# Gates of four row tiles by GpSimd and ScalarE instead of TensorE, and one VectorE step ahead of another

## The chip, the cores and the metric

One core of one Trainium2 chip runs the whole program. The metric is the device time of one execution in microseconds (us). Beside the timed runs there is one profiled execution with a trace. Engines are called PE or TensorE (matmuls), DVE or VectorE, ACT or ScalarE, POOL or GpSimd, and SP, which only issues DMAs.

## The reference

Two sequence layers read the same input `x` (2048 rows of 1024 channels) and are mixed by a gate for each row:

```python
g = sigmoid((x * gate_w).sum(-1, keepdims=True))
a = A(x)      # state space layer: h = Lam_bar * h + B_bar x, y = 2 Re(C h) + x * Dskip
b = B(x, k, v)  # k shifted and weighted by 4 taps, times v, long convolution with ssm_k
                # along the rows (plus ssm_D), times x
return g * a + (1 - g) * b
```

The case is about the first line: for each of the 2048 rows, a sum of 1024 products and two sigmoids, of the sum and of its negative.

## The kernel before

The rows are cut into four blocks `tb` of 512, each of four row tiles `t_` of 128 (0 to 15). The kernel has two halves that overlap.

The first half makes layer B by transforms along the rows, a loop over `c` of eight groups of 128 channels. For each group VectorE multiplies two spectra in a generator, `products(c)`, whose steps are taken one by one with `step` and `steps`: the first step is `first(0)` into `acc`, the second `second(0)` into `wkh` with a gather `acc<-wkh`, the third `first(1)`, the fourth `second(1)`. A "gather" here is a DMA issued by GpSimd that adds its source onto its destination. Between these steps the loop runs the next group's `times_v`: its last step takes `ev = ks - lo` on VectorE and then gathers `ks<-lo`, and the transform `fwd_V` on TensorE reads `ev` and `ks`. At the end of a group `inverse` writes the result to the scratch `cv_scr`.

The second half is the state space layer. `Bu` makes TensorE's input products, `turn_U` rotates them: four ScalarE passes into `Q`, gathered in two gathers into the same tile of `U` (for one group `V`). `scan(tb, g)` runs 16 times (`j = 0..15`) on VectorE. For `j = 8` to `12` the string `plan[j]` gives the output products on TensorE: `Cy_group(tb, g)` adds group `g` into four PSUM tiles, one for each row tile, and after group 3 `scale_a` evicts each tile on ScalarE times the gate (`m<-psy` for block 1, `BT<-psy` for block 2), and `combine` gathers layer B's part onto it. There are four PSUM tiles in all, handed out in turn. The last block's output products follow the loop.

`loads(t_)` loads a row tile's part of layer B (`pbb`) and of `x` (`xr`) on SP's queue; for tiles 12 to 15 `xr` lies in `xlast`. `scale_b(t_)` is two ScalarE passes, `pbb` times `omg` and the `Dskip` row times `gcols`, and a gather. `gcols[:, t_]` holds the gate of a row tile and `omg[:, t_]` one minus it. `gate(tb)` makes them for four row tiles: 32 matmuls of one column with `xT` as weights, then two sigmoids over four columns (`gates_of`). For the last block, `gate(3)` runs at the end of `j = 7`.

What sets the order: `put` chains each instruction of an engine behind the one issued before it, so every engine (GpSimd and SP too) works in the order of the code, and the waits between engines follow from the tiles. Since nearly all instructions go through `put`, they bear its line, L95, in the profile, and are told apart by tile names.

Of the kernel before, what the change touches and what calls it, by code (L numbers as in the profile page):

```python
# [9 lines left out]
ALU = mybir.AluOpType  # L10
ACT = mybir.ActivationFunctionType
BF16 = mybir.dt.bfloat16
F32 = mybir.dt.float32
# [7 lines left out]
def kernel(  # L21
# [26 lines left out]
    nc = tc.nc  # L48
# [4 lines left out]
    S, D = xf.shape  # L53
# [14 lines left out]
    def pool(name, bufs, **kw):  # L68
        return ctx.enter_context(tc.tile_pool(name=name, bufs=bufs, **kw))

    consts = pool("consts", 1)
# [21 lines left out]
    def put(eng, f, *a, **kw):  # L93
        with tc.issue_after(prev[eng]) if eng in prev else nullcontext():
            i = f(*a, **kw)  # L95
        prev[eng] = getattr(i, "ins", i)
# [4 lines left out]
    def bc(ap, shape):  # L101
        return ap.to_broadcast(shape)
# [15 lines left out]
    def act(o, i, **kw):  # L118
        put("act", nc.scalar.activation, out=o, in_=i, **kw)
# [4 lines left out]
    def move(o, i):  # L124
        put("sp", nc.sync.dma_start, out=o, in_=i)
# [670 lines left out]
    def gates_of(c4, sums):  # L796
        act(gcols[:, c4], sums, func=ACT.Sigmoid)
        act(omg[:, c4], sums, func=ACT.Sigmoid, scale=-1.0)

    def gate(tb):  # L800
        psg = ps2([128, 2, 512], "p")[:, 0, 0:4]
        for tl in range(4):
            for dt_ in range(ND):
                mm(psg[:, tl:tl + 1], xTs[tb][:, dt_, tl * 128:(tl + 1) * 128], gwb[:, dt_:dt_ + 1],
                   dt_ == 0, dt_ == ND - 1)
        gates_of(slice(tb * 4, tb * 4 + 4), psg)
# [242 lines left out]
    ios, gas = {}, {}  # L1049
# [5 lines left out]
    def bt_row(g, i):  # L1055

        return BT[g].rearrange("p c d q -> p (c d q)")[:, i * D:(i + 1) * D]
# [60 lines left out]
    def store(t_):  # L1118
        move(rows_of(of, t_), gas.pop(t_))

    def step(gen):
        next(gen, None)

    def run(gen):
        for _ in gen:
            pass

    def steps(gen, n):
        for _ in range(n):
            step(gen)  # L1130
# [41 lines left out]
    tv = times_v(1)  # L1172
# [17 lines left out]
    for c in range(NC - 1):  # L1190
        n, nn = c + 1, c + 2
        if c == 0:
            load("kn", 2)
            load("kT", 2)
            load("v", 2)
            load_BT(0, 0)
            load_xT(0, (1,))
            p1 = products(0, 1)
            fwd_K(n, (0, 1))
            steps(p0, 2)  # L1200
            run(tv)
            dg = dgs(nn, True)
            steps(p1, 2)
            step(p0)
            step(p1)
            run(p0)
            taps(nn, dg)
            step(sp)
            fk = fold_columns(nn)
            step(fk)  # L1210
            fwd_K(n, (2, 3))
            step(p1)
            step(sp)
            fwd_V(n)
            run(p1)
            run(fk)
            tv = times_v(nn)
            step(tv)
            load("kn", 3)
            load("kT", 3)  # L1220
            load_BT(0, 1)
            apart = spread(3)
            step(apart)
            load_xT(0, (0,))
            run(apart)
            continue
        if c == 6:
            put("pool", nc.gpsimd.tensor_copy, stamp, xTs[2][:, 0, 0:HB + 1:HB])
        if c == 6:
            CT[1] = ct_pool.tile([128, 2, D], BF16, name="CT1")  # L1230
            load_CT(1)
            move(rows_, bc(A_Dskip.rearrange("(o d) -> o d", o=1), [128, D]))
        tabs, back, prod = turn_table(c - 1) if c <= NG else none, inverse(c - 1), products(c)
        step(old)
        step(tabs)
        if c == 6:
            step(parts)
        run(back)
        step(tv)
        steps(prod, 4)  # L1240
        run(tv)
        step(old)
        step(tabs)
        run(old)
        fk = none
        if nn < NC:
            dg = dgs(nn)
            if by_channel(nn):
                fk = fold_columns(nn)
                step(fk)  # L1250
        if c == 2:
            step(parts)
        fwd_K(n, (0, 1))
        if c in (2, 6):
            step(parts)
        fwd_K(n, (2, 3))
        if c == 1:
            lam_diag(0, lam_pool, True)
        if c == 4:
            step(parts)  # L1260
        if c == 6:
            run(sp)
            s5p["Q"] = s5p["wu"]
            run(turns_U[2])
            gate(0)
        step(prod)
        if nn < NC:
            if not by_channel(nn):
                fk = mirror_K(nn)
            step(fk)  # L1270
            if c < 5:
                step(fk)
            if c == 4:
                step(parts)
            if c == 1:
                load_BT(1, 0, True)
            elif c in (2, 4):
                load("v", nn, True)
            step(parts)
            taps(nn, dg)  # L1280
            if c == 5:
                load("v", nn)
                load_xT(2, held=True)
            if nn + 1 < NC:
                load("kT", nn + 1, True)
                load("kn", nn + 1)
                apart = spread(nn + 1)
                step(apart)
                if c == 1:
                    load_BT(1, 1)  # L1290
                elif c in (2, 3):
                    load_xT(1, (3 - c,))
                run(apart)
        step(prod)
        run(fk)
        run(prod)
        if n == NC - 1:
            overlap_K(n)
        if nn < NC:
            tv = times_v(nn)  # L1300
            step(tv)
            step(parts)
        else:
            run(next(tiles))
            CT[0] = ld.tile([128, 2, D], BF16, name="CTa", tag="ld")
            hold(CT[0][:, 0, 0:1])
            load_CT(0)
            load_BT(2, 0)
            load_BT(2, 1)
            run(next(tiles))  # L1310
            run(next(tiles))
        fwd_V(n, (0, 1))
        if c < 6 and c != 4:
            step(parts)
            if c in (1, 3):
                step(parts)
        fwd_V(n, (2, 3))
        if c in (4, 5):
            step(parts)
        if c == 1:  # L1320
            lam_diag(1, lam_pool)
        old = tabs

    h3r.close()
    c = NC - 1
# [81 lines left out]
    wk = pool("wk", 2)  # L1407
    s5p["io"] = pool("io", 2)
    s5p["v13"] = pool("v13", 1)

    load_CT(6)
    load_CT(7)
# [44 lines left out]
    def between(j):  # L1457
        for k in multiplied.get(j, ()):
            product(k)
        yield  # L1460
        if j == 3:
            run(turning[6])

    scans = [scan(j // NG, j % NG, between(j)) for j in range(NS)]

    def advance(j):
# [29 lines left out]
    for j in range(NS):  # L1496
        for k in loaded.get(j, ()):
            loads(k)
        if j == 7:
            store(3)  # L1500
        for k in stored.get(j, ()):
            store(k)
        advance(j)
        if j in behind:
            product(behind[j])
        for t in turning[2 * j:2 * j + 2]:
            run(t)
        if j > 0:
            on_act += [lambda t=t: step(t) for t in turning[2 * j + 2:2 * j + 4] for _ in range(4 if j == 1 else 2)]
        turn = turns_U[turned[j]] if j in turned else none  # L1510
        if j != 10 and plan[j][0:1] != "G":
            step(turn)
        by_group = plan[j][0:1] == "G" and j != 10
        if j == 7:
            scale_b(6)
        if by_group:
            for n, k in enumerate(scaled_b.get(j, ())):
                if n == 1:
                    step(turn)
                scale_b(k)  # L1520
            run(turn)
        if j == 4:
            put_off.pop()()
            scale_b(3)
        for unit in plan[j].split():
            if unit == "C0":
                scale_b(2)
            if unit[0] == "G":
                Cy_group(int(unit[1]), int(unit[2]))
            else:  # L1530
                (Bu_next if unit[0] == "B" else Cy_row)(int(unit[1:]))
        if put_off:
            put_off.pop()()
        if j == 10:
            step(turn)
            for k in scaled_b[j]:
                scale_b(k)
            run(turn)
        elif not by_group:
            run(turn)  # L1540
            if j == 5:
                run(turns_U[5])
            for k in scaled_b.get(j, ()):
                scale_b(k)
        if j == 7:
            gate(3)

    for k in at_end:
        product(k)
# [64 lines left out]
```

## Time and profile before

| | |
|---|---|
| median of 3 runs | 379.53 us (379.37 to 379.69) |
| the profiled execution | 379.12 us, of which the span is 377.3 us |
| PE busy | 370.3 us (98%) |
| DVE busy | 367.8 us (97%) |
| ACT busy | 303.9 us (81%) |
| POOL busy | 76.3 us (20%) |
| DMA packets | 70.99 MB, mean 188 GB/s |

Times in the trace are in us from the span's start. A row of a timeline gives the start, the time that it took, the engine, the line, the operation with output and inputs, shapes and count, and in brackets how long the engine stood idle before it and what ended that. A busy time of PE is modelled for pipelined matmuls, so rows overlap a little. A wait for several semaphores is put down to the one that came last by the profile; where the engine named had long been done, it was another, often a DMA. Rows of DMA issues close with the median time from issue to landing; SPq and POOLq are the queues of SP and GpSimd.

### The profile page before, as it was taken

How to read it: one execution, taken by the hardware profiler on the slowest of the kernel's cores; microseconds unless marked ns; L12 is line 12 of the kernel's file. 1: busy time of each engine (PE TensorE's matmuls, PEld its weight loads, DVE VectorE, ACT ScalarE, POOL GpSimd, SP SyncE). 2: the span in 40 equal slices, each digit the busy share in tenths (PEclk: the TensorE clock that was granted, in tenths of full speed). 3: DMA queues.
4: the chain of work that ended last, by engine and by line, in shares of the span. 5: the costliest groups of instructions: out<-in, count | busy, mean ns of one | idle time of the engine just before them, and what ended most of it. 6: DMA issues, size and time to landing. Idle time of an engine off the chain costs nothing.

```text
span 377.3 us, 6661 instructions
## 1 busy us (share of the span) xinstructions
PE 370.3 (98%) x2442; PEld 201.8 (53%) x2477; DVE 367.8 (97%) x596; ACT 303.9 (81%) x465; POOL 76.3 (20%) x106
## 2 busy tenths in 40 slices
PE   8999999999999999999999999999999999999996
PEld 5657567575674847644454444444444444444444
DVE  8999999999999999999999999999999999999975
ACT  5979998988979999687999699978879967946301
POOL 4011030120301203022012013122425323532000
PEclk9999999999999999999999999999999999999999
DMA  7889999999989879998999999746999998996223
GB/s 169 169 141 244 222 219 202 234 217 223 222 188 214 166 167 197 195 202 145 222 210 236 225 197 241 165 75 117 193 240 159 270 247 180 193 248 119 57 83 112
DMA packets 121827, 70.99 MB, mean 188 GB/s; under 512 B 98425, under 2 KB 103425, under 8 KB 121794
## 3 DMA queue, kind: packets, MB, share of 16 engines
q1 hardware_dynamic: 108416, 45.90, 54.6%
q0 software_dynamic: 12256, 24.38, 37.4%
q10 hardware_dynamic: 1122, 0.28, 0.4%
q8 instruction: 19, 0.31, 0.3%
q14 instruction: 14, 0.11, 0.1%
HBM read 16.01 MB, written 8.39 MB: 65 GB/s over the span
## 4 chain that ended last, share of the span: by engine, by line
PE 90%; issue 5%; DMA 3%; SPq 0%; POOL 0%; ACT 0%; DVE 0%; POOLq 0%; ACTq 0%
PE psy L95 29%; PE both L95 22%; PE psk L95 11%; PE psz L95 6%; PE psv L95 6%; PE taps L95 4%; PE foldk L95 4%; PE even L95 3%; PE odd L95 3%; DMA ks<-lo 2%; DMA kT<-in_B_k_dram 1%; PE p L95 1%; PE mirror L95 1%; SPq L95 0%; POOL acc L95 0%
## 5 line engine op out<-in xcount | busy, mean ns | idle before, releaser
L95 PE MATMUL psy<-CT,U 128*128 128x512 bf16 (+1 forms) x418 | 92.7, 374 | 0.4
L95 PEld LDWEIGHTS <-U 128*128 128x128 bf16 x492 | 48.1, 98 | 55.6 <-issue 0.3
L95 PEld LDWEIGHTS <-BT 128*128 128x128 bf16 x544 | 50.5, 98 | 33.5 <-issue 0.2
L95 DVE TENSOR_TENSOR wkh<-BT,Vh 128x2048 bf16<-128x2048 bf16 (+3 forms) x31 | 44.6, 1458 | 0.0
L95 POOL DMA_DIRECT2D U<-Q x26 | 26.6, 1035 | 80.6 <-ACT Q L95 33.0
L95 DVE TENSOR_TENSOR acc<-BT,Vh 128x4096 bf16<-128x4096 bf16 (+3 forms) x19 | 36.9, 1948 | 0.3 <-ACT Vh L95 0.2
L95 ACT ACTIVATE Q<-U,lam 128x512 bf16<-128x512 bf16 (+1 forms) x60 | 35.0, 626 | 1.4 <-issue 1.3
L95 PE MATMUL both<-xT,BT 128*128 128x512 bf16 x157 | 35.2, 379 | 0.2
L95 ACT ACTIVATE Vh<-psv 128x1024 bf16<-128x1024 f32 x32 | 30.6, 1033 | 5.6 <-PE psv L95 5.5
L95 DVE TENSOR_TENSOR_SCAN A<-rv,init,A 128x256 bf16<-128x256 f32 x48 | 34.4, 736 | 0.0
L95 DVE TENSOR_TENSOR acc<-acc,wkh 128x1024 bf16<-128x1024 bf16 (+4 forms) x30 | 32.7, 1128 | 0.1
L95 ACT ACTIVATE BT<-psk 128x1024 bf16<-128x1024 f32 x31 | 30.1, 1046 | 2.3 <-PE psk L95 2.2
L95 ACT ACTIVATE U<-both 128x512 bf16<-128x512 f32 x44 | 24.3, 594 | 8.1 <-PE both L95 7.8
L95 POOL DMA_DIRECT2D acc<-wkh x8 | 9.7, 1218 | 100.7 <-DVE wkh L95 100.7
L95 PEld LDWEIGHTS <-SF 128*128 128x128 bf16 x184 | 18.0, 98 | 19.6 <-issue 0.9
L95 PE MATMUL psk<-eok,SF 128*128 128x384 bf16 (+1 forms) x118 | 28.0, 354 | 0.2
L95 ACT ACTIVATE BT<-psy,gcols 128x1024 bf16<-128x1024 f32 (+1 forms) x6 | 6.3, 1043 | 25.6 <-issue 14.6
L95 PE MATMUL psz<-Vh,CI 128*128 128x512 bf16 x64 | 24.3, 379 | 0.0
L95 PE MATMUL psz<-Vh,SI 128*128 128x512 bf16 x64 | 24.3, 379 | 0.0
L95 PEld LDWEIGHTS <-kT 128*128 128x128 bf16 x352 | 21.5, 101 | 1.6 <-DMA kT<-in_B_k_dram 1.1
L95 PE MATMUL taps<-dg,kT 128*128 128x128 bf16 (+1 forms) x352 | 22.1, 212 | 0.1
L95 DVE TENSOR_TENSOR U<-U,trn 128x512 bf16<-128x512 bf16 (+1 forms) x60 | 22.0, 390 | 0.1
(225 smaller groups left out, 780.1 us busy)
## 6 DMA issues: line engine op xcount, KB each, us to landing
U<-Q POOLq DMA_DIRECT2D x26, 256.0 KB, 4.7
acc<-wkh POOLq DMA_DIRECT2D x6, 768.0 KB, 8.1
cv_scr<-cv SPq DMA_DIRECT2D x16, 256.0 KB, 3.6
kn<-in_B_ssm_k_dram SPq DMA_DIRECT2D x6, 512.0 KB, 3.9
v<-in_B_v_dram SPq DMA_DIRECT2D x2, 1024.0 KB, 6.9
out_dram<-m SPq DMA_DIRECT2D x8, 256.0 KB, 4.2
BT<-cv_scr SPq DMA_DIRECT2D x7, 256.0 KB, 6.0
out_dram<-BT SPq DMA_DIRECT2D x7, 256.0 KB, 2.0
```

Of the source, the lines that this page charges most:

```text
L95: i = f(*a, **kw)
```

## The change

Two edits.

The first is in the loop over `c`: for `c == 5`, the rest of `times_v` (that is, `ev` and the gather `ks<-lo`) runs ahead of the fourth step of `products` and not behind it.

The second takes away `gate(3)`. The row `gate_w` is loaded at the end of `j = 8`, broadcast to 128 partitions, into a room in `BT[0]` that row tile 4 used (`gw_row`). At the end of `j = 9, 10, 11, 12`, GpSimd multiplies the `x` rows of tile 12, 13, 14, 15 with it into `gx`, one f32 tile of 128x1024 that all four share. At the start of the following `j`, ScalarE copies `gx` onto itself with a sum over each row into a column of `gsum`, and `gates_of` makes that tile's two gate columns.

```diff
@@ -1237,7 +1237,10 @@
         run(back)
         step(tv)
-        steps(prod, 4)
+        steps(prod, 3)
+        if c == 5:
+            run(tv)
+        step(prod)
         run(tv)
         step(old)
@@ -1407,6 +1410,9 @@
     s5p["v13"] = pool("v13", 1)
+    gx = pool("gx", 1).tile([128, D], F32, name="gx")
+    gsum = consts.tile([128, 4], F32, name="gsum")
+    gw_row = bt_row(0, 2)
...
+    weighed = {9: 12, 10: 13, 11: 14, 12: 15}
+
     scans = [scan(j // NG, j % NG, between(j)) for j in range(NS)]
@@ -1498,6 +1506,11 @@
         if j == 7:
             store(3)
+        if j - 1 in weighed:
+            t_ = weighed[j - 1]
+            col = gsum[:, t_ - 12:t_ - 11]
+            act(gx, gx, func=ACT.Copy, accum_out=col)
+            gates_of(slice(t_, t_ + 1), col)
         for k in stored.get(j, ()):
             store(k)
         advance(j)
@@ -1542,8 +1555,10 @@
-        if j == 7:
-            gate(3)
+        if j == 8:
+            move(gw_row, bc(gate_w.rearrange("(o d) -> o d", o=1), [128, D]))
+        if j in weighed:
+            put("pool", nc.gpsimd.tensor_tensor, out=gx, in0=ios[weighed[j]][1], in1=gw_row, op=ALU.mult)
```

## The prediction

> **What bounds the kernel now.** I read the page first (busy shares, then the chain that ended last), then the timelines of the engines about the two places that are edited, then the landings of the DMAs there.
>
> ```profile
> span 377.3 us, 6661 instructions
> ...
> PE 370.3 (98%) x2442; PEld 201.8 (53%) x2477; DVE 367.8 (97%) x596; ACT 303.9 (81%) x465; POOL 76.3 (20%) x106
> ...
> PE 90%; issue 5%; DMA 3%; SPq 0%; POOL 0%; ACT 0%; DVE 0%; POOLq 0%; ACTq 0%
> ```
>
> TensorE carries the chain: whatever makes it stand, or takes work off it, moves the end one for one until another engine is late. VectorE is nearly as full. ScalarE and GpSimd have room by their sums, so it is their order, not their load, that has to be read. TensorE's timeline at three places of this case:
>
> ```profile
> 290.28 0.94 PE L95 MATMUL p<-gwb,BT 128*128 128x1 bf16 x32
> ...
> 318.86 1.03 PE L95 MATMUL psy<-CTa,U 128*128 128x512 bf16 x4
> ...
> 346.49 1.03 PE L95 MATMUL psy<-CTa,U 128*128 128x512 bf16 x4
> ```
>
> The first are the gate products that go. The second row starts output block 2 (G20), the third the last block. Each block takes all four PSUM tiles, so its first matmul needs ScalarE to have emptied the tile of row tile 4 (after G13) or 8 (after G23). Neither waits now. On VectorE, the first step that adds row tile 12 to its output:
>
> ```profile
> 366.54 1.28 DVE L95 SCALAR_TENSOR_TENSOR BT<-psy,gcols,xlast 128x1024 bf16<-128x1024 f32 x1 [1.83 <-PE psy L95]
> ```
>
> VectorE waits for TensorE at the end, with at least 1.83 us in hand.
>
> **Part 1, ev ahead of the fourth product step (c = 5).** Nothing is added; ev and then the gather ks<-lo come one product earlier, the product 0.6 us later.
>
> ```profile
> 153.07 0.59 PE L95 MATMUL psv<-ks,SF 128*128 128x512 bf16 x2 [0.84 <-DMA ks<-lo]
> ```
>
> That is the one stall of TensorE in the body, on the landing of the gather.
>
> ```profile
> 143.55 1.75 DVE L95 TENSOR_TENSOR wkh<-BT,Vh 128x3072 bf16<-128x3072 bf16 x1
> 145.22 0.68 DVE L95 TENSOR_TENSOR ev<-ks,lo 128x1024 bf16<-128x1024 bf16 x1
> ```
>
> ```profile
> 141.73 1.20 POOL L95 DMA_DIRECT2D acc<-wkh  x1 [14.97 <-DVE wkh L95]
> 146.21 0.90 POOL L95 DMA_DIRECT2D ks<-lo  x1 [3.27 <-PE psk L95]
> ```
>
> ```profile
> acc<-wkh POOLq DMA_DIRECT2D x1, 768.0 KB, 8.8
> ks<-lo POOLq DMA_DIRECT2D x1, 256.0 KB, 6.8
> ```
>
> The gather would be issued at 146.21 - 1.67 = 144.54. The transfer in front of it in GpSimd's queue lands at 141.73 + 8.8 = 150.5, and the gather at 146.21 + 6.8 = 153.0, 2.5 us after: it stands behind 768 KB either way. The gain lies between 0 and the 0.84 us of the stall; I take 0.1. It counts only if nothing later stops TensorE for longer.
>
> **Part 2a, what goes.** The 32 one-column products of gate(3): 0.94 us of TensorE at 290.28, on the chain, and two small sigmoids. Their PSUM tile also leaves the rotation, which lengthens the distance of the following tiles from their last user: nothing lost. By itself this is -0.94 us.
>
> **Part 2b, what comes, and where it stands.** Four GpSimd products of 128x1024 into one f32 tile gx, four ScalarE sums over it, eight one-column sigmoids, one 256 KB load of gate_w. In the changed order, the product of tile 12 stands on GpSimd behind the second V<-Q gather at j = 9, and its sum on ScalarE stands **ahead of the four m<-psy evictions of block 1**. The products of 13 and 14 stand behind the second U<-Q at j = 10 and 11; the sum of 14 and then scale_b(14) stand ahead of the four evictions of block 2. ScalarE is in order, so those evictions, and TensorE behind them, wait for gathers.
>
> ```profile
> 313.88 1.11 ACT L95 ACTIVATE m<-psy,gcols 128x1024 bf16<-128x1024 f32 x1 [0.41 <-PE psy L95]
> ```
>
> ```profile
> 310.51 1.50 POOL L95 DMA_DIRECT2D V<-Q  x1
> ...
> 319.45 0.86 POOL L95 DMA_DIRECT2D V<-Q  x1 [6.43 <-ACT m L95]
> ```
>
> ```profile
> DMA to landing us min/median/max: 3.3/5.9/8.4
> ```
>
> (The last line is of the two V gathers.) ScalarE is through with the turn at 313.88 - 0.41 = 313.47 and then evicts. But the second V<-Q is not issued before 319.45. The wait named there, ScalarE's m, cannot be it: 310.51 + 8.4 = 318.91, the landing of the first V gather into the same tile, is 0.54 us before it.
>
> The price of a product: no such instruction is in the trace. The nearest GpSimd rows:
>
> ```profile
> 0.98 0.55 POOL L271 IOTA fr__i<- 128x512 int32 x1
> ...
> 2.19 0.46 POOL masks.py:199 TENSOR_SCALAR_AFFINE_SELECT ident<-ident 128x128 bf16<-128x128 bf16 x1
> ```
>
> The DMA share (last but one column) ahead of the first V gather, and one of the sigmoids:
>
> ```profile
> 305.00:310.00 5.00, 4.95 (x23) 2.25 (x23) 5.00 (x13) 2.58 (x4) 0.61 (x2) 1.00 1.13 237
> ```
>
> ```profile
> 295.35 0.19 ACT L95 ACTIVATE gcols<-p 128x4 f32<-128x4 f32 x1
> ```
>
> Twice the iota (written only) is 1.1 us; eight times the select (read and written) is 3.7. I take 2.2, a little over the geometric middle (2.0): two operands are read, but the fixed part of the select is counted eight times. A sum costs one pass of 1.1 us, and two sigmoids with the wait between about 0.35: 1.45 together. The load of gate_w meets full DMA engines (share 1.13, 237 GB/s): 256 KB are 1.1 us, between 0 and that for the first V gather; I take 1.1.
>
> First stall: V gather issued 319.45 + 1.1 + 0.86 = 321.4; product to 323.6; sum and gates to 325.05; eviction 1.11, to 326.15. TensorE wants this tile at 318.86: **+7.3 us**.
>
> Second stall. The U gathers of the next two scans, their landings (300 to 360 us), and ScalarE's passes of such a scan:
>
> ```profile
> 332.60 0.86 POOL L95 DMA_DIRECT2D U<-Q  x1 [6.99 <-ACT Q L95]
> ...
> 333.68 1.62 POOL L95 DMA_DIRECT2D U<-Q  x1
> ...
> 342.17 0.86 POOL L95 DMA_DIRECT2D U<-Q  x1 [5.98 <-issue]
> ```
>
> ```profile
> DMA to landing us min/median/max: 3.4/7.2/9.9
> ```
>
> ```profile
> 320.07 1.32 ACT L95 ACTIVATE Q<-U,lam 128x512 bf16<-128x512 bf16 x2
> 321.30 1.14 ACT L95 ACTIVATE row<-row,omg 128x1024 bf16<-128x1024 bf16 x1
> 322.34 1.13 ACT L95 ACTIVATE gd<-rows,gcols 128x1024 bf16<-128x1024 bf16 x1
> ```
>
> Before, 332.60 - 319.45 = 13.15 us pass for six gathers, V, four m, U, 2.2 each. Now the four m and U follow from 326.15 on: U's landing lets the second U<-Q go at 337.15 and be issued at 338.0. Product 13 to 340.2, sum and gates 341.7, scale_b(12) with two passes of 1.04 to 343.8, the first turn of U15 1.23 to 345.0. The next second gather came 342.17 - 333.68 = 8.5 us after the first as third of four; now it is second of two, 3.4 at least: I take 5.2, so it is issued at 350.25 + 0.86 = 351.1. Product 14 to 353.3, sum and gates 354.75, scale_b(14) 356.85, eviction 357.95. TensorE wants that tile at 346.49, and with the first stall it comes at 353.8: the two stalls make **+11.5 us**. The 0.94 and the 0.1 only make it arrive earlier at the first stall and are lost there.
>
> The products on GpSimd may also hold VectorE: 4 x 2.2 = 8.8 us at most, none at least. TensorE's lateness of 11.5 covers it, with 1.83 on top. VectorE's other tie:
>
> ```profile
> 352.96 0.66 DVE L95 TENSOR_TENSOR U<-U,Q 128x1024 bf16<-128x1024 bf16 x1
> ```
>
> Its Q comes from ScalarE and now follows three more evictions, sum 15 and scale_b(15): 357.95 + 3.3 + 1.45 + 2.1 + 1.2 = 366.0, or +13.0, less the 1.83 in hand +11.2: just under TensorE.
>
> The profiled execution took 379.12 us (377.3 of span, 1.8 around it), 0.41 below the median of 379.53. 379.53 + 11.5 = **391.0 us**.
>
> Bounds: with 1.1 a product, no delay from gate_w and the quickest landings, the second stall falls to +3.7, and the first, +5.1, decides: 384.6. With 3.7 a product (+4.5 over three) and 8.5 for the last gather (+3.3): 398.8.
>
> The Trainium skill, "SBUF — State Buffer", section "Who interferes with whom", says that a VectorE instruction with two SBUF inputs and a GpSimd instruction that reads SBUF exclude each other for a whole instruction. No run shown here has such a pair; by that rule VectorE would lose the whole 8.8 us, and each product would first wait out a VectorE instruction.
>
> **Rivals.** (a) Only the first stall counts: landings are quick once the queue is less full, products cheap, and TensorE meets its second tile free: +5 to +9, at 386.5. For it: the shortest landings, 3.3 and 3.4; against: the medians 5.9 and 7.2.
>
> (b) Longer: each product has to get in between VectorE's back-to-back instructions, such as the 0.66 us U<-U,Q, and the stalled TensorE restarts slowly. Three products wait 0.7 each, 2.1.
>
> ```profile
> 1.19 1.46 PE L95 MATMUL raised<-wkh 128*128 128x512 bf16 x3 [1.19 <-DVE magic L95]
> ```
>
> Three 512-column matmuls at the start, after idleness, take 1.46 us, four in the body 1.03; if about 3 us run so, 1.6 us are lost after the last stall. Together +15.2: 394.7; with dearer products to 400. The page "TensorE: Matmul & The Clock Gate" of the Trainium skill, Part 1, has the same: half rate after an idle window, for one busy window of about 3.4 us.
>
> (c) Faster: ScalarE finds the sum's input ready, nothing stalls, 0.94 to 1.78 us are saved: 378.2 in the middle. That needs product 12 done by 313.47, so the second V gather issued by 310.4, before the first (310.51). It speaks against itself unless the first gather lands in quite another way.
>
> (d) ScalarE unhurt as in (c), but VectorE held for 8.8 us: it has 1.83 in hand before the last block, and TensorE would come 0.94 sooner: 8.8 - 1.83 = 7.0, so 386.5 at most, from 1.83 us of holding on.
>
> (e) The gates end up hidden, stall against saving: no change.
>
> **How the numbers follow.** Forecast (388 to 393) 0.45; (a) 0.21; (b) 0.24; (c) 0.05; (d) 0.03; (e) 0.02. About 0.2% (0.8 us) is what a measurement of this kernel can tell from no change. Faster 0.05, same 0.02, slower 0.93. The range 384 to 398.5 takes in the forecast, (a), (d) and most of (b), and leaves out (c), (e) and the dear end of (b).
>
> **What would show it.** In the profile after: TensorE's first psy matmuls of blocks 2 and 3 with idle time before them, ended by ScalarE's m and BT; ScalarE idle for some 9 us after the turn of Q<-O, released by a GpSimd product of gx; that product starting right after the second V<-Q at about 321; ks<-lo still landing near 153. The forecast is wrong if the product of tile 12 is done before 314, or if TensorE doesn't stand before block 2; its size is wrong if a product takes far from 2.2 us, or if the second block finds its tile free.

## The result and the profile after

| | before | after |
|---|---|---|
| median of the runs beside each other | 379.55 us (6 runs) | 393.24 us (6 runs) |
| the profiled execution | 379.12 us, span 377.3 | 393.92 us, span 392.1 |

The ratio is 1.0336, 95% interval 1.0308 to 1.0364. Here and below, ratios leave disturbed (slow) executions out, so they need not be the quotient of two medians, and the traces of part 1 alone (both) and of the kernel with `gate(0)` moved are of such executions.

Lines of the page of after, and TensorE's waits of the whole run (in total, times, longest):

```profile
span 392.1 us, 6656 instructions
...
PE 373.9 (95%) x2445; PEld 201.3 (51%) x2445; DVE 376.8 (96%) x596; ACT 308.7 (79%) x479; POOL 85.5 (22%) x110
...
DVE 49%; issue 14%; PE 11%; DMA 10%; SPq 7%; ACT 5%; POOL 3%; POOLq 0%; DVEq 0%; ACTq 0%
```

```profile
PE psy L95 <- ACT m L95: 8.0, 1, 8.0
PE psy L95 <- ACT U L95: 2.2, 1, 2.2
PE psy L95 <- ACT BT L95: 1.6, 1, 1.6
PE psv L95 <- DMA ks<-lo: 1.5, 1, 1.5
```

Before, `psy` waited for no one; now it waits 11.8 us. VectorE's busy time is 9.0 us longer with the same 596 instructions. The chain of waits, 90% TensorE before, now is a mixture. TensorE's timeline at the starts of blocks 1, 2 and 3 (before: 291.08, 318.86, 346.49):

```profile
293.49 1.03 PE L95 MATMUL psy<-CTa,U 128*128 128x512 bf16 x4
...
329.30 1.87 PE L95 MATMUL psy<-CTa,U 128*128 128x512 bf16 x4 [8.03 <-ACT m L95]
330.96 1.91 PE L95 MATMUL psy<-CT,U 128*128 128x512 bf16 x4
332.67 1.51 PE L95 MATMUL psy<-CTa,U 128*128 128x512 bf16 x4
334.02 1.03 PE L95 MATMUL psy<-CT,U 128*128 128x512 bf16 x4
...
360.84 1.02 PE L95 MATMUL psy<-CTa,U 128*128 128x512 bf16 x4 [1.62 <-ACT BT L95]
```

The last block starts 14.35 us later than before, and the last output matmuls too. So the loss is made by 360.84. What it was made of is read along GpSimd and ScalarE:

```profile
315.19 1.31 POOL L95 DMA_DIRECT2D V<-Q  x1
...
323.73 0.86 POOL L95 DMA_DIRECT2D V<-Q  x1 [5.60 <-issue]
324.29 2.45 POOL L95 TENSOR_TENSOR gx<-xlast,BT 128x1024 f32<-128x1024 bf16 x1
...
353.62 2.44 POOL L95 TENSOR_TENSOR gx<-xlast,BT 128x1024 f32<-128x1024 bf16 x1
```

```profile
326.77 1.06 ACT L95 ACTIVATE gx<-gx 128x1024 f32<-128x1024 f32 x1 [8.20 <-POOL gx L95]
...
328.16 4.11 ACT L95 ACTIVATE m<-psy,gcols 128x1024 bf16<-128x1024 f32 x4
...
356.09 1.06 ACT L95 ACTIVATE gx<-gx 128x1024 f32<-128x1024 f32 x1 [3.79 <-POOL gx L95]
...
359.69 4.11 ACT L95 ACTIVATE BT<-psy,gcols 128x1024 bf16<-128x1024 f32 x4
```

ScalarE stands 8.20 us for the product of tile 12, with four evictions that need nothing of it queued behind. The same order stands in front of block 3, where ScalarE waits 3.79 us for the product of tile 14 and then does `scale_b(14)` ahead of the evictions.

### The profile page after: what moved, and what is told of

Its sections match the earlier page's. It is cut to its first block, busy times and chain, and to the rows that moved or that the text cites. A ratio compares the mean times of both kernels' runs of the same rounds, so it can differ in the third digit from the quotient of the medians.

```text
span 392.1 us, 6656 instructions
## 1 busy us (share of the span) xinstructions
PE 373.9 (95%) x2445; PEld 201.3 (51%) x2445; DVE 376.8 (96%) x596; ACT 308.7 (79%) x479; POOL 85.5 (22%) x110
## 4 chain that ended last, share of the span: by engine, by line
DVE 49%; issue 14%; PE 11%; DMA 10%; SPq 7%; ACT 5%; POOL 3%; POOLq 0%; DVEq 0%; ACTq 0%
DVE acc L95 18%; DVE wkh L95 12%; SPq L95 7%; PE psy L95 7%; DVE Vh L95 4%; DVE A L95 3%; DVE t L95 3%; DMA xlast<-in_A_x_dram 3%; DVE ks L95 2%; DVE U L95 2%; ACT BT L95 2%; DMA BT<-cv_scr 2%; DMA m<-xr 1%; PE taps L95 1%; DMA pbb<-cv_scr 1%
## 5 line engine op out<-in xcount | busy, mean ns | idle before, releaser
L95 PE MATMUL psy<-CT,U 128*128 128x512 bf16 (+1 forms) x426 | 94.1, 376 | 0.0
L95 PEld LDWEIGHTS <-BT 128*128 128x128 bf16 x512 | 49.6, 98 | 33.2 <-issue 0.2
L95 POOL DMA_DIRECT2D U<-Q x26 | 24.0, 935 | 80.2 <-ACT Q L95 38.7
L95 DVE TENSOR_TENSOR_SCAN A<-rv,init,A 128x256 bf16<-128x256 f32 x48 | 38.6, 824 | 0.0
L95 PE MATMUL psy<-CTa,U 128*128 128x512 bf16 (+1 forms) x66 | 18.1, 396 | 11.9 <-ACT m L95 8.0
```

## The experiments

### Part 2 alone, part 1 alone

Part 2 alone is the changed kernel without the edit at `c == 5`.

> Only part 2: the gates of tiles 12 to 15 by GpSimd and ScalarE, products(5) in the order of before. If ScalarE's sums ahead of the evictions make the loss, TensorE stands 6 to 8.5 us before block 2 with ScalarE's m as releaser, restarts block 3 at 358 to 361 us, and the time is 389 to 392 us. Rival, part 1 makes a good part of the loss by its later landing: 386 to 388 us here.

Measured: 391.33 us, ratio 1.0308 (1.0274 to 1.0342). TensorE's waits for ScalarE are 8.5 us on `m` and 2.1 on `BT`, and block 3 starts at 359.54. Part 2 makes nearly all of the loss.

Part 1 alone is the kernel before with this, run in two comparisons:

```diff
-        steps(prod, 4)
+        steps(prod, 3)
+        if c == 5:
+            run(tv)
+        step(prod)
```

> Only part 1: ev and the gather ks<-lo one product earlier at c = 5; gate(3) stays on TensorE. If the gather stands in GpSimd's DMA queue behind the 768 KB of acc<-wkh, issuing it 1.67 us earlier doesn't land it earlier: it lands at 153 to 154 us, TensorE's stall stays at 0.8 to 1.5 us, and the time is 379.5 to 380.5 us. Rival, the issue time counts: the gather lands at 151.4, the stall of 0.84 us is gone, 378.7 us. Second rival, the 0.8 us later landing seen after the change is multiplied by what follows (DMA transposes, ScalarE waiting for CT<-m, 2.2 us of TensorE before the first psy): 382 us or more.

> Part 1 alone once more (ev and the gather ks<-lo one product earlier at c = 5), beside the kernel with the gather ahead of acc<-wkh. Theory: the gather lands within 1 us of 153, behind the 768 KB, and the ratio is 1.000 to 1.004. Rival (part 1 delays the rest by 2 us, as TensorE's 2.4 us of lateness before block 1 in the changed kernel would have it): ratio 1.005 or more.

Measured: ratios 1.0022 (0.9985 to 1.0059) and 1.0005 (0.9983 to 1.0027). The gather was issued some 1.5 us earlier in both, at 144.79 and 144.62; it landed at 144.79 + 9.3 = 154.1 and at 144.62 + 7.6 = 152.2, against 153.0 before. So the landing scatters about the old one though the issue is earlier each time, and no change of the time can be told. In the changed kernel the landing fell on the late side, at 144.54 + 9.3 = 153.8:

```profile
144.54 0.90 POOL L95 DMA_DIRECT2D ks<-lo  x1 [1.60 <-DVE ev L95]
```

```profile
ks<-lo POOLq DMA_DIRECT2D x1, 256.0 KB, 9.3
```

```profile
153.91 0.59 PE L95 MATMUL psv<-ks,SF 128*128 128x512 bf16 x2 [1.46 <-DMA ks<-lo]
```

### The gather ahead of the 768 KB

The kernel before, with `ev` and the gather `ks<-lo` two products earlier at `c == 5`, and issued before `acc<-wkh`:

```diff
@@ products(c)
             second(0)
+            if c == 5:
+                yield
             gather(A[:, 0, :, 1:], n1[:, 0])
@@ the loop over c
-        steps(prod, 4)
+        if c == 5:
+            steps(prod, 2)
+            run(tv)
+            step(prod)
+        else:
+            steps(prod, 2)
+        steps(prod, 2)
```

> The kernel before with one edit at c = 5: ev and the gather ks<-lo are issued two products earlier and before the 768 KB gather acc<-wkh, so that in GpSimd's queue the order of the two is turned round. Theory (GpSimd's gathers land in the order in which they stand in its queue, so part 1 could gain nothing behind the 768 KB): ks<-lo lands by 147 to 149 us instead of 153 to 154, the 0.84 us stall at 153 goes, acc<-wkh lands some 3 us later; TensorE comes up to 0.84 earlier, though the end may keep only part of it: ratio 0.998 to 1.000. Rival 1 (the gather lands late for its own sake, small rows and full DMA engines): it still lands after 152 and the stall stays. Rival 2 (acc<-wkh, now later, is waited for): a new wait on acc, 1 to 3 us, and slower by 0.3 to 0.8%.

```profile
142.50 0.86 POOL L95 DMA_DIRECT2D ks<-lo  x1 [15.88 <-DVE ev L95]
143.04 1.55 POOL L95 DMA_DIRECT2D acc<-wkh  x1
```

```profile
acc<-wkh POOLq DMA_DIRECT2D x1, 768.0 KB, 10.6
...
ks<-lo POOLq DMA_DIRECT2D x1, 256.0 KB, 5.6
```

It lands at 148.1, 5 us earlier for an issue 3.7 us earlier, and TensorE's stall at 153 is gone. That bears out the prediction's reason, the place in the queue behind 768 KB: from issue to landing the gather took 7.6 to 9.3 us behind the 768 KB with part 1, and 5.6 ahead of them. The time is still the same: 1.0009 (0.9976 to 1.0042). The interval is too wide to exclude the 0.5 us that the profile's span (376.8) shows.

### Other work in that hole

The kernel before, with `gate(0)` moved from `c == 6` into the stall:

```diff
@@ c == 6
             run(turns_U[2])
-            gate(0)
@@ ahead of fwd_V
+        if c == 5:
+            gate(0)
         fwd_V(n, (0, 1))
```

> The kernel before with one edit: the 32 one-column gate products of the first 512 rows, gate(0), and their sigmoids are issued at c = 5 in front of the backward products, where TensorE stood 0.84 us for the gather ks<-lo, instead of at c = 6. Neither gx nor the gather's place changes. Theory (the gather lands with GpSimd's queue, whatever TensorE does; what is done in the wait is free): the stall at 153 goes or shrinks to 0.1, and the time falls by 0.7 to 0.9 us, ratio 0.998. Rival 1 (TensorE's lead at c = 5 is lost at the next tie, the wait for ScalarE or VectorE by 250 us, or at the end): no change, 1.000 within 0.001. Rival 2 (the gates' PSUM tile or their sigmoids, now earlier, push a ScalarE step of that turn): slower by 0.3 to 1 us, with a ScalarE wait in the rows behind 153.

The stall is gone there too (the 32 one-column products run in it, 0.94 us), and the ratio is 0.9998 (0.9975 to 1.0021). A gain of 0.8 us would just lie within that interval; what is shown is only that it isn't larger.

### What the removal saves

The kernel before without `gate(3)`; the gates of the last four row tiles are not computed, they get those of the four tiles before.

> gate(3) is left out and nothing is put in its place: tiles 12 to 15 get the gate columns of block 2 (so the gates of the last 512 rows are not computed). Prices the removed matmuls by themselves. If they are on the chain one for one: 0.94 us less, 378.6 us. Rival, VectorE or a DMA takes the end over: 379.3 to 379.5 us.

Measured: ratio 0.9974 (0.9944 to 1.0005), so 1.0 us, uncertain by 1.2: the -0.94 of the prediction fits, though the interval just takes in no gain at all. So much, about 1 us, is to be had by taking these products off TensorE with nothing put in their place.

### The products alone

The kernel before with the load of `gate_w` and the four GpSimd products, without the sums, and with `gate(3)` kept. ScalarE's order is then as before.

> gate(3) stays and makes the gates; the load of gate_w and the four GpSimd products of part 2 are added at their places, their result is not used, and there are no sums on ScalarE. If the order on ScalarE makes the loss, TensorE doesn't stand before block 2 or 3. What is left is VectorE, held about 2 us by each product (2.0 to 2.4 us in the trace after): 8 us late at the end, of which its idle time at the end covers some 4: 381 to 384 us. Rival, the hold of VectorE is the loss: 388 us or more.

Measured: 386.81 us, ratio 1.0188 (1.0154 to 1.0222), beyond the 381 to 384 that I had expected and short of the rival's 388. In the last 90 us TensorE no longer waits for ScalarE but for VectorE, and VectorE has no wait left at the end:

```profile
PE psy L95 <- DVE U L95: 2.9, 2, 2.5
```

GpSimd's third product, and VectorE's timeline through it and the fourth:

```profile
345.06 4.60 POOL L95 TENSOR_TENSOR gx<-xlast,BT 128x1024 f32<-128x1024 bf16 x1
```

```profile
346.94 0.75 DVE L95 TENSOR_TENSOR A<-A,trn 128x512 bf16<-128x512 bf16 x2
347.61 2.47 DVE L95 TENSOR_SCALAR A<-V,lam 128x512 bf16<-128x512 bf16 x2
350.00 3.93 DVE L95 TENSOR_SCALAR trn<-V,lam 128x512 bf16<-128x512 bf16 x2
```

Each pair of `TENSOR_SCALAR` took 0.61 us before. The product issued at 345.06 waits through VectorE's back-to-back two-input instructions until 347.61, then VectorE stands until it is over. A product of 2.44 us so becomes 4.60, and VectorE loses 1.9 us (2.47 instead of 0.61). The page "SBUF — State Buffer" of the Trainium skill, section "Who interferes with whom", has this as a lock held for a whole instruction; the runs agree on VectorE's side, and show on GpSimd's that the wait can be several VectorE instructions, not one.

### One stall taken out

Part 2 alone, with the sum of tile 12 behind the evictions of block 1:

```diff
-        if j - 1 in weighed:
+        if j - 1 in weighed and j != 10:
             gate_of(weighed[j - 1])
@@ behind the last put-off eviction
+        if j == 10:
+            gate_of(12)
```

(`gate_of` is the sum and the two sigmoids.)

> Part 2 alone, with one edit: the ScalarE sum of tile 12 and its two sigmoids are queued behind the four evictions m<-psy of block 1 instead of ahead of them; the sum of tile 14 and scale_b(14) stay ahead of the evictions of block 2. Theory (one chain: GpSimd's products and gathers set when the second stall ends, and TensorE's lateness there is the larger of the two): the stall of 8 to 8.5 us before block 2 goes, but the gathers behind product 12 stay late, the stall before block 3 grows from about 2 to 5 us or more, and the time is 386 to 390 us, 2 to 5 below part 2 alone. Rival 1 (the two stalls add, each its own): the stall before block 3 stays at about 2 us and the time falls by about 8, to 383. Rival 2 (VectorE takes over): TensorE hardly waits for ScalarE any more, VectorE, held some 8 to 10 us by the products as with the products alone, is busy to the end and the time is 386 to 387 whatever the stalls do. Theory and rival 2 are told apart by what ends TensorE's waits in the last 40 us: ScalarE's BT, or VectorE's U.

Measured: 391.46 us, ratio 1.031 (1.0279 to 1.0342), just as with both stalls:

```profile
356.67 1.87 PE L95 MATMUL psy<-CTa,U 128*128 128x512 bf16 x4 [9.28 <-ACT BT L95]
...
360.03 1.05 PE L95 MATMUL psy<-CTa,U 128*128 128x512 bf16 x4
```

The stall before block 2 is gone and the one before block 3 grew from 2.1 to 9.28 us, ended by `BT` and not by VectorE. So the stalls don't add: the chain over GpSimd's gathers and products decides when block 3 may start. Block 3 starts 2.9 us earlier than with part 2 alone (359.54), but now TensorE comes out of the long idleness and takes 6.84 us for the first 24 matmuls instead of 5.17: of the 2.9 us, 1.7 are given back there, and the span falls by 1.2. My theory had the mechanism and not this; its 2 to 5 us did not come.

### The products earlier

Part 2 alone, with each product in front of the second gather of its turn:

```diff
             for k in scaled_b.get(j, ()):
                 scale_b(k)
+            if j in (9, 11):
+                weigh(weighed[j])
             run(turn)
```

(and likewise for `j = 10`; the last one stays at the end of `j = 12`).

> Part 2 alone, with the GpSimd products moved in front of the second gather of their turn (they stood behind it); the sums stay where they are on ScalarE, in front of the evictions. GpSimd stood idle for 6 to 8 us between the two gathers of a turn. Theory: product 12 ends near 321 rather than 326.7, its sum near 322.5, so the stall before block 2 falls from 8.5 to about 4 us (the gather behind it comes up to 2.4 us later only if the product isn't over by the time that it could go), the stall before block 3 stays under 2 us, and the time is 385 to 388 us, VectorE's hold of 8 to 10 us setting the floor. Rival (the wait is for VectorE, not for the queue of gathers): a product issued earlier only waits longer for an instruction of VectorE that lets it in, it ends at the same time as before and the time stays at 390 to 392 us.

Measured: 385.19 us, ratio 1.0135 (1.0097 to 1.0172).

```profile
313.34 4.22 POOL L95 TENSOR_TENSOR gx<-xlast,BT 128x1024 f32<-128x1024 bf16 x1
```

```profile
315.50 2.47 DVE L95 TENSOR_SCALAR A<-U,lam 128x512 bf16<-128x512 bf16 x2
```

```profile
PE psy L95 <- DVE U L95: 2.1, 2, 1.7
PE psy L95 <- ACT m L95: 1.8, 1, 1.8
```

Product 12 is done at 317.6 rather than 325.3, the wait on `m` falls from 8.5 to 1.8 us, that on `BT` goes, and about 6 us come back. The rival (a product only waits for VectorE longer) falls.

The next step puts the sums of 12 and 14 and `scale_b(14)` behind the evictions as well:

> As the kernel before it in this list (part 2 alone, products ahead of the second gather), and the sums of tiles 12 and 14 with their sigmoids, and scale_b(14), are queued behind the four evictions of the block instead of ahead. No eviction waits for a product any more. Theory: TensorE has no stall on ScalarE's m or BT over 1 us; what is left is VectorE, whose instructions the products hold for 8 to 10 us in sum, less the 1.83 us that it had in hand and less the 0.94 us of gate products: 379.5 + 6 = 385 to 387 us, as with the products alone (386.8) less up to 0.9. Rival (the hold of VectorE hides as long as ScalarE's order is good): 379 to 381 us, no slower than before by more than 0.5%.

Measured: 386.2 us, ratio 1.0153 (1.0108 to 1.0198). TensorE has no wait for ScalarE's `m` or `BT` left, and the time gains nothing more: VectorE bounds the end, as with the products alone.

### How much of VectorE's time a product costs

The same placement as in the kernel with 385.19 us, with products and sums over 512 columns:

```diff
-                weigh(weighed[j])
+                weigh(weighed[j], 512)
```

> Part 2 with the products in front of the second gather (385.2 us), and each product and sum over 512 of the 1024 columns; half of each of the four gates' sums is left out. Theory (what is left of the loss is VectorE standing while a product runs: 1.9 to 2.5 us for each full one, held from the moment it is let in): the products take about 1.2 us, hold VectorE 0.7 to 1.3 each, 3 to 5 us in sum instead of about 9, and the time falls by 3.5 to 5 us, to 380 to 382. Rival (each product costs VectorE a fixed price, and ScalarE its sums and sigmoids, whatever their width): less than 1.5 us better, 383.7 or more.

Measured: 381.56 us, ratio 1.0067 (1.0035 to 1.0098). `TENSOR_SCALAR` is held for less:

```profile
315.79 1.51 DVE L95 TENSOR_SCALAR A<-U,lam 128x512 bf16<-128x512 bf16 x2
```

That is 0.9 us of hold instead of 1.9, in three of the four products; the remaining one, that of tile 13, held 1.8 instead of 2.5. The hold goes with the product's length. The last control gives GpSimd the same time without reading an operand, in the products-only kernel:

```diff
-        put("pool", nc.gpsimd.tensor_tensor, out=gx, in0=ios[t_][1], in1=gw_row, op=ALU.mult)
+        for h in (0, 512, 0, 512):
+            put("pool", nc.gpsimd.iota, gx[:, h:h + 512], pattern=[[4, 512]], base=1, channel_multiplier=0)
```

> The products-only kernel (386.8 us; no sums, gate(3) kept) with each GpSimd product replaced by four iotas of 128x512 int32 into the same place, 4 x 0.55 = 2.2 us of GpSimd without any operand read; nothing uses them. Theory (a product with two operands in SBUF excludes VectorE's two-input instructions, an iota doesn't): VectorE's instructions keep their lengths, and the time is 379.5 to 381, as before but for the load of gate_w and later gathers. Rival 1 (GpSimd's time in front of the gathers is what costs): 385 to 387 as with the products. Rival 2 (any GpSimd instruction that writes SBUF holds VectorE): its instructions show holds of 0.5 us or more at the iotas, and the time is 383 or more.

Measured: 381.77 us, ratio 1.0067 (1.0041 to 1.0094), between theory and rivals.

```profile
336.50 2.21 POOL L95 IOTA gx<- 128x512 int32 x4
...
345.30 2.40 POOL L95 IOTA gx<- 128x512 int32 x4
```

```profile
336.30 1.38 DVE L95 TENSOR_TENSOR_SCAN A<-rv,init,A 128x256 bf16<-128x256 f32 x2
337.60 0.66 DVE L95 TENSOR_TENSOR U<-U,A 128x1024 bf16<-128x1024 bf16 x1
...
345.35 3.22 DVE L95 TENSOR_SCALAR A<-V,lam 128x512 bf16<-128x512 bf16 x2
```

Scans and two-input instructions beside iotas keep their lengths (1.38 and 0.66 as before); `TENSOR_SCALAR` is held for 2.6 us, and a `CAST` took 0.88 us instead of 0.16. So rival 1 (GpSimd's time as such, 385 to 387) falls as the whole price, and reading the operands is what makes most of the products' price; my theory that iotas leave VectorE alone was wrong for one kind of instruction. The section of the Trainium skill named above has both cases: two-input instructions meet only GpSimd's reads, `tensor_scalar` and casts can meet its writes too. This run agrees.

VectorE's busy time above that of before (367.8), less the 1.83 us that it had in hand there, against how much longer the span was:

| kernel | VectorE busy, more | less 1.83 | span, more |
|---|---|---|---|
| iotas | 3.4 | 1.6 | 2.9 |
| half products, in front | 4.3 | 2.5 | 2.1 |
| products in front | 8.1 | 6.3 | 5.5 |
| in front, sums behind | 8.3 | 6.5 | 7.2 |
| products alone | 9.6 | 7.8 | 7.0 |

The last two columns agree to 0.8 us, but for the iotas, with 1.3; there VectorE also waited 1.38 us for a gather `U<-Q` (at 341.60), which it did in none of the other four nor before (from 300 us on), and 1.6 + 1.4 is 3.0. Wherever ScalarE's order is not the bound, the hold on VectorE fits the price. No version with products or iotas beat the kernel before.

## Why the prediction was right, point by point

The forecast was 391.0 us in 384 to 398.5; the median is 393.24. It lies just above the 388 to 393 that the forecast had for itself, and nearer to the 394.7 of rival (b). The mechanism is still the forecast's, as the next points show; what made the time longer was neither of (b)'s two terms, but a lateness ahead of the first stall.

**Order and mechanism.** Each step named is there: ScalarE idle after the turn (8.20 us, forecast some 9), released by the product of `gx`; the product right behind the second `V<-Q`; TensorE idle ahead of blocks 2 and 3, ended by `m` and `BT`.

**First stall.** The eviction was to end at 326.15, and TensorE started at 329.30, 3.15 us later. One term was mis-sized: the delay of the second `V<-Q`, put at 1.1 us for the load of `gate_w`, so an issue at 320.55; it was issued at 323.73, 4.28 us after that of before. The other terms held: product 2.45 (2.2), sum and gates from 326.77 to 328.16, 1.39 (1.45), eviction 1.14 (1.11). The 4.28 can be followed along GpSimd's queue. Of the two gathers `U<-Q` ahead of the V gathers, the second was issued 0.5 us after the landing of the first (before: 299.90 and 309.39):

```profile
302.52 1.55 POOL L95 DMA_DIRECT2D U<-Q  x1
...
313.88 0.86 POOL L95 DMA_DIRECT2D U<-Q  x1 [8.61 <-ACT gd L95]
```

The first came 2.62 us later than before, and the second followed after 11.36 us instead of 9.49, 1.87 more, since the first landed 10.8 us after its issue instead of 9.0; the steps from there to the second `V<-Q` took 0.21 less. In the seven other kernels with the load the two are 10.0 to 10.8 us apart, in two without it 8.4 and 9.5. So the 1.1 us for the load was about right in size, though no run has the load alone. The larger part was there before it: TensorE came 2.41 us later into block 1, which the prediction had put at nothing, with this wait 100 us behind the edit of part 1:

```profile
252.05 1.02 PE L95 MATMUL psy<-CTa,U 128*128 128x512 bf16 x4 [2.20 <-ACT U L95]
```

ScalarE had stood 3.41 us for the gather `CT<-m` ahead of it. Whether part 1 causes this is open. Both traces of part 1 alone have that wait of ScalarE (6.1 and 6.0 us), but so has the one with `gate(0)` moved (4.1), without part 1; the kernel with part 2 alone and the late sum shows TensorE's wait, 1.25 us, also without part 1; and part 1 alone moved the time by no more than its interval. The profiled execution is 0.7 us above the median, so not all of this lateness need be in every execution.

**Second stall.** From the end of product 12 to the end of the eviction ahead of block 3 I had 357.95 - 323.6 = 34.35 us; to TensorE's start it took 360.84 - 326.74 = 34.1. The links between are near their sizes (to the end of product 13 17.1 for 16.6, from there to the start of product 14 9.8 for 10.9, and from there 7.2 for 6.85), so the lateness of 2.9 us at block 3 is the one of the first stall handed on. That the larger lateness counts and not the sum of two stalls is shown by the run with the sum of tile 12 moved.

**Part 1** was put at -0.1 us: no gain behind 768 KB. No gain was found, and the gather ahead of them bears out the reason; the stall that part 1 was to shorten even grew in the changed kernel, from 0.84 to 1.46.

**Part 2a**, -0.94 us, was said to be lost ahead of the first stall. Its size fits the removal alone (-1.0, uncertain by 1.2).

**Cover for VectorE.** I had at most 8.8 us of hold, covered by TensorE's lateness. VectorE's timeline in the changed kernel, with the `CAST` of before for comparison:

```profile
322.63 0.16 DVE L95 CAST WL<-A 128x4 f32<-128x4 bf16 x1
```

```profile
324.67 2.10 DVE L95 CAST WL<-A 128x4 f32<-128x4 bf16 x1
...
341.25 3.12 DVE L95 TENSOR_TENSOR_SCAN A<-rv,init,A 128x256 bf16<-128x256 f32 x1
...
353.72 2.90 DVE L95 TENSOR_TENSOR O<-O,A 128x1024 bf16<-128x1024 bf16 x1
...
362.24 3.25 DVE L95 TENSOR_TENSOR_SCAN A<-rv,init,A 128x256 bf16<-128x256 f32 x2
369.29 0.69 DVE L95 TENSOR_TENSOR U<-U,Q 128x1024 bf16<-128x1024 bf16 x1 [3.80 <-ACT Q L95]
```

Less their usual 0.16, 0.74, 0.66 and 1.38 these are 8.4 us. It is covered: VectorE still waits 3.80 us for `Q` at 369.29. With the cover gone it costs about what rival (d) said: 386.5 at most, and the products alone took 386.81.

**Bounds.** The prediction's lower bound has +3.7 for the second stall. From 11.5, three products cheaper by 1.1, no 1.1 for the load and 3.4 instead of 5.2 for the last landing give +5.3; it isn't said which landing makes the rest. The bound would be 384.8 instead of 384.6.

**Rivals.** (a), only the first stall: its lateness at block 2, 10.4 us, was passed on, and block 3 waited again. (b), longer: its slow restart is real, but cost nothing at the end, since block 3 waited for ScalarE anyway. Its other half, products waiting for VectorE, was nearly nothing here (they took 2.44 to 2.66 us, against 2.43 at the least in any kernel with 1024 columns), and up to 2.5 us each in the kernels where they met rows of two-input instructions. (c) and (e) fall.

## What to carry to other kernels

Where an engine works in the order of the code, ask of each added instruction what stands behind it that doesn't need it: the four sums cost ScalarE under 6 us, but two of them held evictions, and so TensorE, for the landing of gathers. Moving an engine's work to a less busy one is no relief if that one holds up a third that is nearly full: 0.94 us saved on TensorE was paid with 8 us on a VectorE that had 1.83 in hand. And a stall that is taken away shows its worth only at the next tie of the chain; here it came back whole in front of the next block.

## What the runs showed of the hardware that was not expected

**A slow restart.** TensorE's granted clock in the changed kernel about the first stall (each row gives the stretch, its length, the busy times of PE, PEld, DVE, ACT and POOL, the clock, the DMA share and GB/s):

```profile
322.00:326.00 4.00, 0.00 (x0) 0.00 (x0) 4.00 (x7) 0.00 (x0) 2.27 (x2) 0.68 0.39 69
326.00:329.00 3.00, 0.00 (x0) 0.00 (x0) 2.96 (x9) 2.19 (x5) 0.74 (x1) 0.50 0.19 32
...
331.00:333.00 2.00, 2.00 (x6) 0.72 (x5) 2.00 (x4) 2.00 (x4) 1.71 (x3) 0.50 1.06 180
...
334.00:335.00 1.00, 1.00 (x6) 0.49 (x5) 1.00 (x3) 1.00 (x2) 0.63 (x1) 1.00 1.13 190
```

It fell to 0.50 within the idleness and came back only between 333 and 334, over 4 us after the restart: 2.1 us lost over the first 24 matmuls (7.31 us instead of 5.17). After the stall of 1.62 us nothing was lost. The page "TensorE: Matmul & The Clock Gate" of the Trainium skill, Part 1, has some 3.4 us for the way back; the run with the late sum agrees (356.67 to 360.03), this one took longer.

**Who gets in.** In four kernels, GpSimd products that were issued where VectorE ran `TENSOR_TENSOR` back to back waited for up to 2.5 us (4.60 and 4.93 us instead of 2.44); all but one of those that waited over 1 us got in when a `TENSOR_SCALAR` came. Yet this is no rule: others got in at once, ahead of a scan, a `CAST` or also a `TENSOR_TENSOR`, as this product and the VectorE row that it held in the kernel with 385.19 us:

```profile
327.23 2.43 POOL L95 TENSOR_TENSOR gx<-xlast,BT 128x1024 f32<-128x1024 bf16 x1
```

```profile
327.06 3.23 DVE L95 TENSOR_TENSOR A<-A,trn 128x512 bf16<-128x512 bf16 x2
```

What decides whether a product gets in between two `TENSOR_TENSOR` is not shown.
